# Weight tiles of their own, modulation weights on two queues, and three w1 loads moved ahead of the value copies

## The chip, the cores and the metric

The kernel runs on one core of a Trainium2 chip. The metric is device time in microseconds of one execution. The engines are named as in the profile: PE (TensorE matmul) and PEld (its weight loads), DVE (VectorE), ACT (ScalarE), POOL (GpSimd) and SP (SyncE, which issues nearly all DMAs of this kernel).

## What is computed

One block with adaptive layernorm: S = 2048 tokens of D = 512 features in bfloat16, a local attention with 32 heads of 16 features whose window has 8 positions with a step of 2, and an MLP that mixes tokens, with F = 1792.

```python
mod = (_silu(c) @ w_mod).reshape(c.shape[0], 6, 1, -1)   # sa, ca, ga, sb, cb, gb
h = _layernorm(x) * (1 + ca) + sa
x = x + ga * _A_ref(h, A_wqkv, A_wo)
h = _layernorm(x) * (1 + cb) + sb
x = x + gb * _B_ref(h, B_w1, B_b1, B_w2, B_b2)

# _A_ref: q, k, v from x @ wqkv;  idx = pos - [0, 2, ..., 14], masked where negative
logits = jnp.einsum('bhsd,bhswd->bhsw', q, kg) * scale
o = jnp.einsum('bhsw,bhswd->bhsd', _softmax(logits), vg)      # then @ wo
# _B_ref: u = gelu(einsum('bsd,sf->bdf', layernorm(x), w1) + b1);  y = einsum('bdf,fs->bds', u, w2) + b2
```

## The kernel before

The tokens are worked in four chunks of 512 (`build_chunk`, chunk 0 to 3), each of four tiles of 128 tokens. Of each chunk: layernorm (statistics on DVE, then `rstd`: a logarithm into `lv` and an exponential into `rs` on ACT, then `nb` on DVE, then `n_sb`, on DVE or ACT), a transpose on PE, the modulation of the transposed tile into `hTb` (named hT below; its columns `sacol` and `a1col` come from matmuls with one column each on the modulation weights), then 48 matmuls for query, key and value with the weights as stationary operand. Their results are evicted from PSUM into `q_sb`, `k_c` and `v_c` by ACT or DVE.

The attention multiplies elementwise on DVE: four products `prod` of query and shifted key of each chunk, and four products `pvb` of the softmax weights `a2sb` and the value. For the latter the values lie four times in `vD`, shifted; 16 DMAs of 32 x 2104 elements copy them there out of `v_c` in each chunk, 8 of each half. `vD` has three buffers. The sums over features and positions are matmuls with constant matrices (`group`, `stack`). Then come the output projection, the residual, a second and a third layernorm, and `h3`.

The MLP's first matmuls take w1 in seven blocks of 256 columns (`fc` 0 to 6) and in two levels: level 0 works with the tokens of chunks 0 and 1 and parks its sums in `gT`, level 1 with chunks 2 and 3. A block of one level is 512 KB. Level 0 loads them in turn into four buffers `wst`, which first hold the modulation rows; so its blocks 4 to 6 are loaded when blocks 0 to 2 have been used. Level 1 takes dead space: `w_raw`, `hTb`, and two of `wst`. The second matmuls take w2 in eight blocks of 896 KB, loaded into dead attention buffers.

All loads but one go through SP's queue, which works in order. A wait of one DMA on its buffer holds all that stand behind it.

Nothing here is written in the order in which it runs. Each step is an operation of a graph with engines, durations and dependences; a planner (`_Graph.schedule`) walks through it with a model of the engines and of one DMA pipe, chooses among ready operations by a table of priorities (`PRI`, a number for each kind of step and chunk), and between ACT and DVE by the earlier end, with a penalty `DB` on DVE. The code is then written in that order. Every instruction is recorded at one helper line, L208, so that the profile's groups are told apart by tile names.

The weights for query, key and value lie in one tile, columns `t * D` to `(t + 1) * D` of each of four rows of blocks:

```python
w_raw = T([P, KT, 3 * D], BF, "w_raw")
load(w_raw[:, :, t * D:(t + 1) * D], wqkv_view[:, :, t * D:(t + 1) * D], ...)
lhsT = _ap(w_raw[:, kt, t * D + j: t * D + j + 1], [[4, P]])
```

Key and query loads are held by a tiny copy on DVE (`hold_w`) until the statistics of a token tile are there. PE runs 13 matmuls on a constant (`warm`) at the start.

Of the kernel before, what the change touches and what calls it, by code (L numbers as in the profile page):

```python
# [9 lines left out]
BF = mybir.dt.bfloat16  # L10
# [3 lines left out]
P = 128  # L14
# [243 lines left out]
def kernel(  # L258
# [13 lines left out]
    PRI=(("ln1s", (-13773, -14814, 4735, 3582)), ("rstd1", (-14433, 1324, -6172, 2750)),  # L272
         ("nb1", (-13688, -10031, 8315, 26112)), ("ln1n", (12276, 4360, 29028, 55658)),
         ("tr", (-27269, -16160, 5273, -11182)), ("hT", (-31581, -17745, 20709, -3603)),
         ("qkvk", (-10761, -39897, -10907, 28658)), ("qkvq", (36465, 12433, 33335, 19673)),
         ("qkvv", (23004, -1542, 56675, 39121)), ("evk", (-39675, -52214, -12496, 12715)),
         ("evq", (-2536, -6788, 16753, 3144)), ("evv", (13543, -6355, 34438, 27036)),
         ("khalo", (5854, -5148, 3210, 20138)), ("vhalo", (13698, 20720, 49158, 39104)),
         ("vd", (9675, -10333, 32741, 40101)), ("qk", (6637, 9160, 33741, 41660)),
         ("red", (-7058, -688, 36723, 23347)), ("max", (-21689, -24379, -17972, 13331)),  # L280
         ("sub", (-28150, -8660, 6329, 38993)), ("exp", (-23987, -14379, 2772, 8798)),
# [15 lines left out]
    DB: float = 0.4,  # L297
# [4 lines left out]
    WARM: int = 13,  # L302
# [5 lines left out]
    G.XLAT = 0.06  # L308
    C = 512
# [16 lines left out]
    def T(shape, dtype, name):  # L326
        return sb.tile(shape, dtype, name=name)
# [13 lines left out]
    w_raw = T([P, KT, 3 * D], BF, "w_raw")  # L341
# [98 lines left out]
    dma(wmodA, wmod_view[:, :, 0:2 * D], 2 * D * D * 2, [], vdk[0], "ld_wmodA")  # L440
# [10 lines left out]
    def load_w(t):  # L451
        load(w_raw[:, :, t * D:(t + 1) * D], wqkv_view[:, :, t * D:(t + 1) * D], D * D * 2, [], [("w", t)], f"ld_w{t}")

    def later_loads():

        for (t, st) in ((1, 1), (0, 3)):
            add("dve", 0.07, lambda t=t, st=st: nc.vector.tensor_copy(w_raw[:, 0, t * D:t * D + 1],
                                                                      mv[0][0][:, st, 0:1]),
                reads=[("mv0", 0, st)], writes=[("w", t)], name=f"hold_w{t}", lat=0.1, pk=-200.0)
            load_w(t)  # L460
# [125 lines left out]
    def build_chunk(ch):  # L586
# [82 lines left out]
        for (t, j0, j1) in plan:  # L669
# [3 lines left out]
            def f(t=t, j0=j0, n=n, sq=sq):  # L673
                for jj in range(n):
                    j = j0 + jj
                    for kt in range(KT):
                        lhsT = _ap(w_raw[:, kt, t * D + j: t * D + j + 1], [[4, P]])
# [19 lines left out]
        for hfd in range(2):  # L697
# [4 lines left out]
            for dh2 in range(2):  # L702
                for w4 in range(4):
# [4 lines left out]
                        [("vD", vs, w4, dh2)], f"vd{ch}_{hfd}{w4}{dh2}", rate=220.0)  # L708
# [190 lines left out]
    ctr_ws = [0]  # L899
# [149 lines left out]
```

## Time and profile before

| | us |
|---|---|
| median of 3 runs | 228.72 (228.63 to 230.21) |
| profiled execution | 229.2 |
| its span, first to last instruction | 227.2 |
| PE busy | 201.3 (89%) |
| DVE busy | 164.3 (72%) |
| ACT busy | 112.7 (50%) |
| mean granted clock of PE | 0.962 |

The profiled execution lies 2.0 us above its span. Times of rows are counted from the span's start. Busy time of PE is that of records whose ends are modelled, and matmuls overlap, so a busy PE may still do less than it could; a row's time of several matmuls divided by their number is the better measure. In a row with "idle before", the idle time is that of its engine, and the name behind the arrow is what the profile holds for the cause.

### The profile page before, as it was taken

How to read it: one execution, taken by the hardware profiler on the slowest of the kernel's cores; microseconds unless marked ns; L12 is line 12 of the kernel's file. 1: busy time of each engine (PE TensorE's matmuls, PEld its weight loads, DVE VectorE, ACT ScalarE, POOL GpSimd, SP SyncE). 2: the span in 40 equal slices, each digit the busy share in tenths (PEclk: the TensorE clock that was granted, in tenths of full speed). 3: DMA queues.
4: the chain of work that ended last, by engine and by line, in shares of the span. 5: the costliest groups of instructions: out<-in, count | busy, mean ns of one | idle time of the engine just before them, and what ended most of it. 6: DMA issues, size and time to landing. Idle time of an engine off the chain costs nothing.

```text
span 227.2 us, 3338 instructions
## 1 busy us (share of the span) xinstructions
PE 201.3 (89%) x1267; PEld 92.1 (41%) x1288; DVE 164.3 (72%) x225; ACT 112.7 (50%) x208; POOL 4.0 (2%) x27
## 2 busy tenths in 40 slices
PE   6639999979599999948999957999999999999993
PEld 2314553444245343413344313444444444444452
DVE  4562799998899999999995758996643344555444
ACT  2423985095987979773575924895653200000000
POOL 7000000000000000000000000000000000000000
PEclk9956999999999999976999999999999999999999
DMA  4899777899640000019999999999992011011111
GB/s 153 273 357 288 227 154 129 171 165 225 170 122 0 3 0 0 3 52 165 162 165 243 190 248 278 292 290 290 293 248 74 23 49 46 29 40 46 49 46 46
DMA packets 41555, 32.96 MB, mean 145 GB/s; under 512 B 1988, under 2 KB 38980, under 8 KB 41540
## 3 DMA queue, kind: packets, MB, share of 16 engines
q1 hardware_dynamic: 41532, 32.75, 61.1%
q8 instruction: 10, 0.16, 0.4%
q14 instruction: 5, 0.04, 0.1%
q10 hardware_dynamic: 8, 0.00, 0.0%
HBM read 22.03 MB, written 2.10 MB: 106 GB/s over the span
## 4 chain that ended last, share of the span: by engine, by line
PE 38%; DVE 16%; DMA 10%; issue 2%; SPq 0%; DVEq 0%
PE ps L208 38%; DMA vD<-v_c 10%; DVE pvb L208 6%; DVE h L208 3%; DVE prod L208 2%; DVE st L208 2%; DVE nm L208 1%; DVE mv L208 0%; SPq L208 0%; DVE k_c L208 0%; DVE va L208 0%; DVEq L208 0%; DVE nb L208 0%
## 5 line engine op out<-in xcount | busy, mean ns | idle before, releaser
L208 PE MATMUL ps<-hTb,w_raw 128*128 128x512 bf16 x184 | 46.1, 395 | 4.4 <-DVE st L208 2.3
L208 DVE TENSOR_TENSOR pvb<-a2sb,vD 128x4096 bf16<-128x4096 bf16 x16 | 36.0, 2288 | 7.9 <-DMA vD<-v_c 4.2
L208 PEld LDWEIGHTS <-w_raw 128*128 128x128 bf16 x240 | 25.9, 112 | 33.1 <-issue 8.5
L208 PE MATMUL ps<-h,wst 128*128 128x512 bf16 x139 | 33.8, 392 | 3.0 <-ACT h L208 2.2
L208 DVE TENSOR_TENSOR prod<-q_sb,k_c 128x4096 bf16<-128x4096 bf16 x16 | 36.0, 2285 | 0.0
L208 PEld LDWEIGHTS <-wst 128*128 128x128 bf16 x144 | 13.9, 100 | 22.0 <-issue 7.9
L208 PE MATMUL ps<-gT,vD 128*128 128x512 bf16 x82 | 18.2, 379 | 0.1
L208 PE MATMUL ps<-woq,o_sb 128*128 128x512 bf16 x63 | 16.2, 379 | 0.0
L208 PEld LDWEIGHTS <-vD 128*128 128x128 bf16 x132 | 10.5, 97 | 14.0 <-DMA vD<-in_w_mod_dram 2.0
L208 DVE SCALAR_TENSOR_TENSOR q_sb<-ps,b2col,gb_bc 128x512 f32<-128x512 f32 x8 | 6.0, 751 | 12.6 <-PE ps L208 12.6
L208 DVE SCALAR_TENSOR_TENSOR k_c<-ps,b2col,gb_bc 128x512 f32<-128x512 f32 (+1 forms) x9 | 6.2, 692 | 11.4 <-PE ps L208 11.4
L208 PEld LDWEIGHTS <-o_sb 128*128 128x128 bf16 x106 | 10.3, 98 | 9.9 <-issue 0.4
L208 PE MATMUL ps<-pvb,stack 128*32 128x512 bf16 x128 | 9.9, 384 | 4.1 <-DVE pvb L208 4.1
L208 PE MATMUL ps<-prod,group 128*32 128x512 bf16 x128 | 10.1, 398 | 2.7 <-DVE prod L208 2.5
L208 PE MATMUL ps<-gT,prod 128*128 128x512 bf16 x55 | 12.3, 379 | 0.1
L208 DVE BATCH_NORM_STATS2 st<-xx 128x6 f32<-128x512 bf16 x16 | 10.7, 671 | 2.1 <-DMA xx<-in_A_x_dram 2.1
L208 PE MATMUL ps<-gT,pvb 128*128 128x512 bf16 x55 | 12.2, 379 | 0.1
L208 ACT ACTIVATE k_c<-ps 128x1024 bf16<-128x1024 f32 (+1 forms) x9 | 8.3, 925 | 7.9 <-PE ps L208 7.8
L208 DVE BATCH_NORM_STATS2 st<-h 128x6 f32<-128x512 bf16 x16 | 10.9, 679 | 0.0
L208 PE MATMUL ps<-h,w_raw 128*128 128x512 bf16 x48 | 10.8, 379 | 0.0
L208 ACT ACTIVATE xx<-ps 128x512 bf16<-128x512 f32 x16 | 9.4, 587 | 2.3 <-PE ps L208 1.6
L208 ACT ACTIVATE v_c<-ps 128x1024 bf16<-128x1024 f32 x8 | 8.0, 1017 | 4.6 <-PE ps L208 3.2
(95 smaller groups left out, 242.7 us busy)
## 6 DMA issues: line engine op xcount, KB each, us to landing
vD<-v_c SPq DMA_DIRECT2D x64, 131.5 KB, 5.4
wst<-in_B_w_dram SPq DMA_DIRECT2D x9, 512.0 KB, 7.5
vD<-in_B_w_dram SPq DMA_DIRECT2D x3, 896.0 KB, 10.6
wst<-in_w_mod_dram SPq DMA_DIRECT2D x4, 512.0 KB, 8.5
prod<-in_B_w_dram SPq DMA_DIRECT2D x2, 896.0 KB, 9.8
pvb<-in_B_w_dram SPq DMA_DIRECT2D x2, 896.0 KB, 8.7
w_raw<-in_A_wqkv_dram SPq DMA_DIRECT2D x3, 512.0 KB, 4.8
xx<-in_A_x_dram SPq DMA_DIRECT2D x3, 512.0 KB, 7.7
```

What stands on the lines that cost most here:

```text
L208: r = fn(*a, **k)
```

## The change

Each of the three weights gets a tile of its own (`w_q`, `w_k`, `w_v`). The first load of modulation weights is cut in two halves of 512 KB: one stays in SP's queue, the other is issued on ACT's. The copies that hold the key and query loads are put first on DVE. Level 0's w1 blocks 4 to 6 are loaded into `w_q`, `w_k` and `w_v`, after the last query, key and value matmuls; level 1 takes `wst` for blocks 0 to 3, `hTb` for 4 and 5 and `w_q` for 6. There are 15 warm-up matmuls instead of 13. All of the priorities have new values, DVE's penalty falls from 0.4 to 0.2, and the planner's model of DMAs gets a longer fixed time and a lower rate of value copies.

```diff
-    PRI=(("ln1s", (-13773, -14814, 4735, 3582)), ("rstd1", (-14433, 1324, -6172, 2750)),
+    PRI=(("ln1s", (-62333, -28891, -1164, 11138)), ("rstd1", (-33229, 4350, 3857, 26221)),
...
-    DB: float = 0.4,
+    DB: float = 0.2,
...
-    WARM: int = 13,
+    WARM: int = 15,
...
+    G.DMA_FIXED = 2.2
...
-    w_raw = T([P, KT, 3 * D], BF, "w_raw")
+    w_p = [T([P, KT, D], BF, f"w_{n}") for n in "qkv"]
...
-    dma(wmodA, wmod_view[:, :, 0:2 * D], 2 * D * D * 2, [], vdk[0], "ld_wmodA")
+    dma(wmodA[:, 0:2, :], wmod_view[:, 0:2, 0:2 * D], 2 * D * P * 2 * 2, [], vdk[0][4:], "ld_wmodA", "act",
+        behind=[G.ops[-1]])
+    dma(wmodA[:, 2:4, :], wmod_view[:, 2:4, 0:2 * D], 2 * D * P * 2 * 2, [], vdk[0][:4], "ld_wmodB")
...
-        load(w_raw[:, :, t * D:(t + 1) * D], wqkv_view[:, :, t * D:(t + 1) * D], D * D * 2, [], [("w", t)], f"ld_w{t}")
+        load(w_p[t][:], wqkv_view[:, :, t * D:(t + 1) * D], D * D * 2, [], [("w", t)], f"ld_w{t}")
...
-            add("dve", 0.07, lambda t=t, st=st: nc.vector.tensor_copy(w_raw[:, 0, t * D:t * D + 1],
+            add("dve", 0.07, lambda t=t, st=st: nc.vector.tensor_copy(w_p[t][:, 0, 0:1],
                                                                       mv[0][0][:, st, 0:1]),
-                reads=[("mv0", 0, st)], writes=[("w", t)], name=f"hold_w{t}", lat=0.1, pk=-200.0)
+                reads=[("mv0", 0, st)], writes=[("w", t)], name=f"hold_w{t}", lat=0.1, pk=-1e6)
...
-                        lhsT = _ap(w_raw[:, kt, t * D + j: t * D + j + 1], [[4, P]])
+                        lhsT = _ap(w_p[t][:, kt, j:j + 1], [[4, P]])
...
-                        [("vD", vs, w4, dh2)], f"vd{ch}_{hfd}{w4}{dh2}", rate=220.0)
+                        [("vD", vs, w4, dh2)], f"vd{ch}_{hfd}{w4}{dh2}", rate=170.0)
...
-            if last and fc < 5:
...
-                w = ctr_ws[0] % NWS
-                ctr_ws[0] += 1
-                w1p = wst[w][:, 0:nst, :]
-                wk, w = [("wst", w)], ("wst", w)
+            spare = (fc - 4 if fc >= 4 else None) if not last else {4: 3, 5: 4, 6: 0}.get(fc)
+            if spare is None:
+                w1p, wk = wst[fc][:, 0:nst, :], [("wst", fc)]
+            else:
+                src_ = w_p[spare][:].rearrange("p a b -> p (a b)") if spare < 3 else (
+                    hTb[:, spare - 3, :, :].rearrange("p a b -> p (a b)"))
+                w1p = src_.rearrange("p (a b) -> p a b", b=EW)[:, 0:nst, :]
+                wk = [("w", spare)] if spare < 3 else [("hT", spare - 3, kt) for kt in range(KT)]
...
-                behind=last_vd[-16:] if last else (), after=last_qkv[-6:] if last and fc < 5 else (), rate=290.0)
+                behind=last_vd[-16:] if last else (), after=last_qkv[-6:] if spare is not None else (), rate=290.0)
```

Three places in the order of the built program. Buffer numbers are shifted by two by the new tiles. First DVE at the start, from the end of the first chunk's statistics to its first modulated tiles (`hTb`); before:

```order
L208 SCALAR_TENSOR_TENSOR nb_0_138<-mv_0_122,rs_0_132 128x2
L208 CAST w_raw<-mv_0_122 128x1 x2
L208 COPY vD_89<-sc 128x512
L208 SCALAR_TENSOR_TENSOR nb_0_138<-mv_0_122,rs_0_132 128x2
L208 COPY sacol<-ps_63 128x4
L208 TENSOR_SCALAR a1col<-ps_63 128x4
L208 TENSOR_SCALAR n_sb<-xx,rs_0_132,nb_0_138 128x512 x2
L208 TENSOR_SCALAR hTb<-ps_64,a1col,sacol 128x512 x2
```

The same place after the change, from the third tile's statistics on:

```order
L208 CAST w_k<-mv_0_124 128x1
L208 BN_STATS st_0_120<-xx 128x6
L208 BN_AGGR mv_0_124<-st_0_120 128x2
L208 SCALAR_TENSOR_TENSOR nb_0_140<-mv_0_124,rs_0_134 128x2
L208 CAST w_q<-mv_0_124 128x1
L208 TENSOR_SCALAR n_sb<-xx,rs_0_134,nb_0_140 128x512 x2
L208 SCALAR_TENSOR_TENSOR nb_0_140<-mv_0_124,rs_0_134 128x2
L208 COPY vD_91<-sc 128x512
L208 COPY sacol<-ps_63 128x4
L208 TENSOR_SCALAR a1col<-ps_63 128x4
L208 TENSOR_SCALAR hTb<-ps_64,a1col,sacol 128x512 x2
```

DVE's two normalizations move from behind the copies of the modulation columns to ahead of them, and the copies that hold the key and query loads stand apart and earlier.

Second ACT, from the first chunk's normalizations to the second chunk's `lv`, `rs` and `n_sb`; before:

```order
L208 ACTIVATE n_sb<-xx,nb_0_138,rs_0_132 128x512 x2
L208 ACTIVATE hTb<-ps_61,sacol,a1col 128x512 x2
L208 ACTIVATE k_c_74<-ps_62 128x512
L208 ACTIVATE k_c_74<-ps_63 128x512
L208 ACTIVATE k_c_74<-ps_64 128x2x512
L208 ACTIVATE q_sb_72<-ps_61 128x512
L208 ACTIVATE k_c_75<-k_c_74 128x4x16
L208 ACTIVATE lv_1_127<-mv_1_123,epscol 128x4
L208 ACTIVATE rs_1_133<-lv_1_127 128x4
L208 ACTIVATE n_sb<-xx,nb_1_139,rs_1_133 128x512 x3
```

After the change:

```order
L208 ACTIVATE n_sb<-xx,nb_0_140,rs_0_134 128x512 x2
L208 ACTIVATE hTb<-ps_61,sacol,a1col 128x512 x2
L208 ACTIVATE k_c_76<-ps_62 128x512
L208 ACTIVATE k_c_76<-ps_63 128x512
L208 ACTIVATE k_c_76<-ps_64 128x2x512
L208 ACTIVATE k_c_77<-k_c_76 128x4x16
L208 ACTIVATE lv_1_129<-mv_1_125,epscol 128x4
L208 ACTIVATE rs_1_135<-lv_1_129 128x4
L208 ACTIVATE v_c_78<-ps_61 128x2x512
L208 ACTIVATE n_sb<-xx,nb_1_141,rs_1_135 128x512 x4
```

The query eviction (`q_sb`) between the key evictions and the second chunk's `lv` is gone from there, and a value eviction stands behind `rs`.

Third SP's queue around the value copies of chunks 2 and 3 (`vD<-v_c`; `wst`, `w_raw` and `w_q` to `w_v` from in_B_w are w1 blocks); before:

```order
L208 DMA vD_88<-v_c_77 32x2104 x8
L208 DMA vD_89<-v_c_76 32x2104 x8
L208 DMA vD_90<-v_c_76 32x2104 x8
L208 DMA vD_88<-v_c_77 32x2104 x7
L208 DMA wst_96<-in_B_w_dram 128x8x256
L208 DMA vD_88<-v_c_77 32x2104
L208 DMA wst_97<-in_B_w_dram 128x8x256
L208 DMA vD_89<-v_c_77 32x2104 x6
L208 DMA wst_98<-in_B_w_dram 128x8x256
L208 DMA vD_89<-v_c_77 32x2104 x2
L208 DMA w_raw<-in_B_w_dram 128x8x256 x3
```

After the change:

```order
L208 DMA vD_90<-v_c_79 32x2104 x8
L208 DMA w_q<-in_B_w_dram 128x8x256
L208 DMA w_k<-in_B_w_dram 128x8x256
L208 DMA w_v<-in_B_w_dram 128x8x256
L208 DMA vD_91<-v_c_78 32x2104 x8
L208 DMA vD_92<-v_c_78 32x2104 x8
L208 DMA vD_90<-v_c_79 32x2104 x8
L208 DMA vD_91<-v_c_79 32x2104 x8
L208 DMA wst_98<-in_B_w_dram 128x8x256
```

Three w1 loads move from between the copies of chunk 3 to ahead of the copies of chunk 2. The first row of each piece is the second half of chunk 1.

## Rows read from the trace of the kernel before

**Rows 1.** Windows, four stages: length, PE, PEld, DVE, ACT, POOL busy, clock, DMA share, GB/s.

```profile
0.00:23.80 23.80, 16.22 (x88) 7.30 (x90) 10.13 (x32) 8.55 (x17) 4.03 (x27) 0.78 0.88 272
23.80:111.00 87.20, 77.40 (x597) 36.30 (x605) 84.45 (x96) 63.73 (x113) 0.00 (x0) 0.96 0.52 104
111.00:138.00 27.00, 22.56 (x182) 8.93 (x187) 20.00 (x12) 15.23 (x29) 0.00 (x0) 1.00 1.10 211
138.00:223.50 85.50, 85.11 (x407) 39.62 (x408) 48.84 (x84) 25.16 (x51) 0.00 (x0) 1.00 0.51 135
```

**Rows 2.** Timeline of the start: start us, us, engine, operation [idle before <-releaser].

```profile
7.17 0.92 SPq L208 DMA_DIRECT2D w_raw<-in_A_wqkv_dram  x2
...
7.51 1.50 ACT L208 ACTIVATE n_sb<-xx,nb,rs 128x512 bf16<-128x512 bf16 x2
...
9.13 0.95 PE L208 MATMUL ps<-sc,vD 128*128 128x1 bf16 x32 [1.54 <-DMA vD<-in_w_mod_dram]
...
10.12 0.16 DVE L208 COPY sacol<-ps 128x4 f32<-128x4 f32 x1 [2.32 <-PE ps L208]
...
10.26 0.73 DVE L208 TENSOR_SCALAR n_sb<-xx,rs,nb 128x512 bf16<-128x512 bf16 x2
...
12.01 1.45 ACT L208 ACTIVATE hTb<-ps,sacol,a1col 128x512 bf16<-128x512 bf16 x2 [3.00 <-PE ps L208]
...
13.05 0.59 PE L208 MATMUL ps<-hTb,w_raw 128*128 128x512 bf16 x1 [1.08 <-DMA w_raw<-in_A_wqkv_dram]
...
15.97 0.15 PEld L208 LDWEIGHTS <-w_raw 128*128 128x128 bf16 x2 [2.84 <-DMA w_raw<-in_A_wqkv_dram]
...
17.56 0.18 DVE L208 BATCH_NORM_AGGREGATE mv<-st 128x2 f32<-128x6 f32 x1
...
21.72 1.02 ACT L208 ACTIVATE k_c<-ps 128x1024 bf16<-128x1024 f32 x1 [1.93 <-PE ps L208]
22.64 0.59 ACT L208 ACTIVATE q_sb<-ps 128x512 bf16<-128x512 f32 x1
23.11 0.26 ACT L208 ACTIVATE k_c<-k_c 128x64 bf16<-128x64 bf16 x1
23.26 0.30 ACT L208 ACTIVATE lv<-mv,epscol 128x4 f32<-128x4 f32 x1
...
23.83 0.16 DVE L208 SCALAR_TENSOR_TENSOR nb<-mv,rs 128x4 f32<-128x4 f32 x1 [5.29 <-ACT rs L208]
```

**Rows 3.** Windows of the start, columns as in rows 1.

```profile
7.60:10.40 2.80, 1.27 (x40) 1.25 (x40) 0.44 (x4) 1.41 (x3) 0.00 (x0) 1.00 0.75 245
10.40:20.60 10.20, 6.36 (x22) 2.50 (x21) 5.50 (x14) 2.64 (x4) 0.00 (x0) 0.50 1.11 327
```

**Rows 4.** Timeline of PE, the last w1 blocks.

```profile
167.94 7.07 PE L208 MATMUL ps<-h,wst 128*128 128x512 bf16 x32
```

**Rows 5.** Timeline of DVE, the last four value products.

```profile
124.56 4.50 DVE L208 TENSOR_TENSOR pvb<-a2sb,vD 128x4096 bf16<-128x4096 bf16 x2 [2.71 <-ACT a2sb L208]
130.97 2.29 DVE L208 TENSOR_TENSOR pvb<-a2sb,vD 128x4096 bf16<-128x4096 bf16 x1 [1.91 <-DMA vD<-v_c]
135.54 2.29 DVE L208 TENSOR_TENSOR pvb<-a2sb,vD 128x4096 bf16<-128x4096 bf16 x1 [2.28 <-DMA vD<-v_c]
```

**Rows 6.** SP's queue: two w1 loads; issue to landing of wst, 110 to 180 us.

```profile
125.35 0.53 SPq L208 DMA_DIRECT2D wst<-in_B_w_dram  x1
...
149.40 3.04 SPq L208 DMA_DIRECT2D wst<-in_B_w_dram  x1
...
DMA to landing us min/median/max: 8.6/10.2/11.7
```

**Rows 7.** Windows around the value copies, columns as in rows 1.

```profile
90.00:99.00 9.00, 7.01 (x43) 3.27 (x44) 8.76 (x16) 7.56 (x17) 0.00 (x0) 1.00 0.01 2
...
103.00:115.00 12.00, 11.44 (x85) 4.62 (x86) 11.90 (x16) 5.19 (x8) 0.00 (x0) 0.88 1.05 160
136.00:146.00 10.00, 8.06 (x43) 3.56 (x43) 9.09 (x16) 6.12 (x16) 0.00 (x0) 1.00 1.09 282
```

More of the change, by code (lines that the diff above doesn't have):

```diff
@@ L271 @@
     out: bass.AP,
-    PRI=(("ln1s", (-13773, -14814, 4735, 3582)), ("rstd1", (-14433, 1324, -6172, 2750)),
[L273 to L281, printed above, removed]
[11 rows of a table removed]
+    PRI=(("ln1s", (-62333, -28891, -1164, 11138)), ("rstd1", (-33229, 4350, 3857, 26221)),
+         ("nb1", (-35128, -10199, 606, 61630)), ("ln1n", (-13250, -779, 43561, 82136)),
+         ("tr", (-42262, -34195, 20572, -3461)), ("hT", (-50005, -19470, 30352, 9017)),
+         ("qkvk", (-4121, -22202, -18413, 51700)), ("qkvq", (32552, 14395, 18838, 32017)),
+         ("qkvv", (12501, 10460, 80919, 50056)), ("evk", (-22227, -27999, -13500, 34769)),
+         ("evq", (-21544, 751, 504, 4679)), ("evv", (33896, 8448, 60640, 52635)),
+         ("khalo", (3373, -999, 15697, 32477)), ("vhalo", (15160, 31777, 58416, 57816)),
+         ("vd", (15555, 6823, 48214, 59794)), ("qk", (15175, 12857, 42871, 54449)),
+         ("red", (4921, -7740, 48749, 42783)), ("max", (-40383, -24565, -6786, 7476)),
+         ("sub", (-31386, -8103, 37482, 40474)), ("exp", (-35480, -16607, -2144, 1231)),
[11 rows of a table added]
     MK: int = 1000,
@@ L897, in chained @@
         return op
-    ctr_ws = [0]
     bounds = [0] + list(LEVELS) + [NST]
@@ L909 @@
         for fc in range(F // EW):
-            if last and fc < 5:
-                w = ("wr", fc)
-                src_, off = (w_raw, fc * 2048) if fc < 3 else (hTb, (fc - 3) * 2048)
-                w1p = src_[:].rearrange("p a b -> p (a b)" if fc < 3 else "p a b n -> p (a b n)")[
-                    :, off:off + nst * EW].rearrange("p (a b) -> p a b", a=nst)
-                wk = [("w", fc)] if fc < 3 else [("hT", fc - 3, kt) for kt in range(KT)]
-                w = wk[0]
-            else:
-                w = ctr_ws[0] % NWS
-                ctr_ws[0] += 1
-                w1p = wst[w][:, 0:nst, :]
-                wk, w = [("wst", w)], ("wst", w)
+            spare = (fc - 4 if fc >= 4 else None) if not last else {4: 3, 5: 4, 6: 0}.get(fc)
+            if spare is None:
+                w1p, wk = wst[fc][:, 0:nst, :], [("wst", fc)]
+            else:
+                src_ = w_p[spare][:].rearrange("p a b -> p (a b)") if spare < 3 else (
+                    hTb[:, spare - 3, :, :].rearrange("p a b -> p (a b)"))
+                w1p = src_.rearrange("p (a b) -> p a b", b=EW)[:, 0:nst, :]
+                wk = [("w", spare)] if spare < 3 else [("hT", spare - 3, kt) for kt in range(KT)]
+            w = wk[0]
             dma(w1p, w1_view[:, s_lo:s_hi, fc * EW:(fc + 1) * EW], P * nst * EW * 2, [], wk, f"ld_w1_{li}_{fc}",
-                behind=last_vd[-16:] if last else (), after=last_qkv[-6:] if last and fc < 5 else (), rate=290.0)
+                behind=last_vd[-16:] if last else (), after=last_qkv[-6:] if spare is not None else (), rate=290.0)
             sm = G.slot("ps")
```

22 rows, old and new, of the table PRI are left out of this document.

## The prediction

> **What bounds the kernel now.** I read the windows view first, because a share of busy time over the whole span mixes stages with different limits. The reader is to see four stages [rows 1]. Up to 23.8 us nothing is full: PE is busy for 16.22 us, at a mean granted clock of 0.78, and DVE for 10.13. From 23.8 to 111 DVE is busy for 84.45 of 87.2 us: it is the bound. From 111 to 138 neither is full (PE 22.56 and DVE 20.00 of 27), while the DMA engines are. From 138 on PE is busy for 85.11 of 85.5 us at full clock. So a gain must come from the first stage, which sets when the DVE stage begins, or from the third, which sets when the last matmuls may begin; what is saved there moves everything behind it, as long as DVE and PE find their inputs.
>
> Then the timeline of the start [rows 2], for what ends last. The first query-key-value matmul starts at 13.05 behind a DMA into w_raw, and the next weight load waits for another one until 15.97. SP issued the key and the query weights from 7.17, then a part of x, then the value weights. While the clock is low the DMA moves 327 GB/s [rows 3], 1.6 us for each of these 512 KB loads. If the wait at 13.05 is for the second (query) load, the key weights had landed at 11.4; two loads later, at 16.2, the value weights land, which is where the second wait ends. So the key matmuls wait for weights that they don't read: all three lie in one tile, and the column sets of the three interleave in it. What follows is a chain on ACT, which works in order: the third key eviction at 21.72, a query eviction, the halo copy, and only at 23.26 the logarithm for the second chunk's layernorm, whose statistics DVE had ready at 17.74. DVE idles 5.29 us for it, until 23.83.
>
> Last, DVE at the end of the attention [rows 5]: its last two value products wait 1.91 and 2.28 us for value copies (vD<-v_c). SP's queue [rows 6] has three w1 loads between those copies; the last of them, at 125.35, is shown.
>
> **The change, part by part.**
>
> *Start, term A.* Three edits work on it. The normalizations of tiles 2 and 3 stood on DVE behind the copy of the modulation columns (10.12, then 10.26) and now stand on ACT, which doesn't wait for those columns. They can begin there when DVE has done the two other tiles (0.73 us, in the place of ACT's two from 7.51) and the second bias step, near 8.3, and take 1.50: done at 9.8. The transposes then follow the modulation matmuls, which end at 10.08, without a break: 16 in some 1.2 us, and the last two hT on ACT, 1.45 us in before, end near 12.8 instead of 13.46. The key tile is there by then (11.4), so the 16 key matmuls run from about 12.4 with no wait. At full clock (2.4 GHz) one takes 0.22 us, 32 of them 7.07 [rows 4], so they end at 15.9; at 1.2 GHz they take 0.44 each and end at 19.4. In before the third eviction could start at 21.72. From there to the logarithm go 0.92 us of the eviction and 0.15 of the halo copy's step; the query eviction between them is now later in ACT's order. So the logarithm could start at 17.1 (full clock) or 20.5 (low clock), against 23.26. It can't start ahead of the second chunk's statistics, which are done at 17.74 if x lands as now, and up to some 0.9 us earlier if the loads, whose two holding copies now come earlier on DVE, move up. So A is between 5.5 and 6.2 at full clock, 2.8 at the low one. I take 6.0, for the full clock: the low one began at 10.4 after a stretch with 1.27 us of PE work in 2.8 [rows 3], and this stretch is now shortened from both sides, by two more warm-up matmuls ahead and by earlier transposes behind.
>
> A must not be lost again in the DVE stage. DVE has 84.45 us of work there; by the order of the changed kernel it takes on one more query eviction (0.69) and one hT (0.53), and gives up three normalizations of 0.4 and one more of h: nothing, within 0.4 us. The new table of priorities moves many other instructions between neighbouring places, but on an engine without idle time that changes no sum.
>
> *Modulation weights on two queues.* The DMA of 1 MB lands just before 9.13. It is now two halves; the one on ACT is issued behind the table load, that is near 2.7 instead of 1.8 us. I count nothing: the trace has no such split, and the bounds are -0.9 us (the late issue is paid in full) and +1.5 (PE's idle time before 9.13 goes). The Trainium skill, "DMA: Bandwidth & Descriptors", section "Issuing engines are not separate DMA queues", says that transfers from several issuing engines share the same 16 DMA engines, so that a second queue saves only issue time. By that rule this part gives nothing, by the hope behind a second queue it would give the 1.5.
>
> *Three w1 loads out of the value copies, term B.* Loads of w1 and w2 alone move 282 GB/s, value copies alone 160 GB/s, both with the DMA share over 1 [rows 7]. A w1 load of 512 KB is then 1.86 us, three are 5.6; a value copy of 32 x 2104 elements is 0.84. The copies of the last two chunks run as one full stretch, so without the three loads the last ones land 5.6 us earlier. The two waits of DVE, 1.91 + 2.28 = 4.19, are shorter than that and go; then DVE itself is late next, with four products of 2.29 us in a row. B is 4.2. The wait of 2.71 us before the first of the four is for ACT's copy of the attention weights and stays.
>
> The loads go into the tiles of the query, key and value weights. SP now issues them ahead of the copies of chunk 2, and everything behind them in SP's queue waits with them: the value copies of chunks 2 and 3. The last matmuls that read the query and key tiles come before the last value matmuls of chunk 2, on which those copies wait anyhow, so only the third load (1.86 us) can stand in their way, and the DMA is idle there: 2 GB/s from 90 to 99 us [rows 7]. I count 0; if the cover is gone, 1.9 us to all of B.
>
> *The last stage.* It has the same matmuls. One load is read earlier than before: the fourth w1 block of the second half. In before its place in SP's queue (issued at 149.40) was that of the sixth block. It takes part in rival 3.
>
> **Sum.** The profiled execution has a span of 227.2 us and took 229.2; the median of the three runs is 228.72, so the profile is 0.5 us above it, less than I can resolve. 229.2 - 6.0 - 4.2 = 219.0 us.
>
> **The rivals.**
>
> 1. *The clock falls at the start all the same.* For: the modulation matmuls have one column each and the transposes are short, and in before just this work let the clock go from 1.00 to 0.50 [rows 3]. Against: the pause gets shorter. A is 2.8 instead of 6.0: 222.2 us.
>
> 2. *The loads are still in the way of the copies.* If the value tile comes free late, or SP is held at the first load, all 5.6 us lie ahead of chunk 2's copies instead of within chunk 3's. The last copy lands as before relative to the DVE work, B is 0: 223.2. Against it stands the idle DMA.
>
> 3. *The fourth w1 block comes late, and it gets slower.* In before, 32 matmuls were left when PE came to the last two blocks at 167.94 [rows 4]; in the new order 56 are left when it comes to the fourth, so this point is at 167.94 - 24 x 0.22 - 10.2 = 152.4. Its place in SP's queue was issued at 149.40, and such loads took 8.6 to 11.7 us from there to landing [rows 6]. If place and time don't move, it lands at 159.6 in the median, and PE waits 7.2 us in the one stage where it is the bound. There the clock would fall as at the start: 10.2 us at 0.50 [rows 3] is 5.1 us of matmuls. Together 12.3: 231.3. The price begins with a landing at 152.4, and from 157.5 on the kernel is slower than before. Against it: the queue ahead is shorter by the three loads (5.6) and starts earlier by A, so the load should land near 148, with 4 us in hand.
>
> 4. *The change doesn't free the key matmuls.* If the wait until 15.97 was truly for the key weights, the 16 matmuls begin there and end at 19.5, as at low clock: A is 2.7 and the time 222.3.
>
> **How the numbers follow.** The forecast has 0.60, rival 1 0.22, rival 2 0.09, rival 3 0.03, rival 4 0.06. The likeliest case gives 219.0. The range reaches down to 229.2 less 7.7 (A with the 1.5 of an earlier modulation) less 4.2 less the 0.5 between profile and median, 216.8, and up past rivals 1, 2 and 4 to 224.0, which leaves room for 1 to 2 us of lost cover in two of them. About 1% is what a measurement of this kernel can tell from no change, 226.4 to 231.0. Only rival 3, and rivals 1 and 2 together with more lost cover, come near it: faster 0.94, same 0.04, slower 0.02.
>
> **What would show it.** A is right if the key matmuls start before 13 us and run through, if no DMA into a weight tile is named before them, and if DVE's 5.29 us are gone, so that the first value product starts some 6 us earlier. The clock in the stretch from 10 to 21 us tells the forecast from rival 1. B is right if the last four value products follow each other without a DMA wait; rival 2 if such waits show at chunk 2's or the last ones; rival 3 if PE waits for a DMA into wst after its last attention work. The forecast is wrong if DVE is found idle between 20 and 110 us by more than the 2.8 us of now, for then the new order has starved it and A is lost in the middle.

## The result, and the profile after

The changed kernel took 221.99 us in the median of four executions (221.25 to 226.06), beside 229.47 us (228.63 to 231.53) of the kernel before. The forecast of 219.0 is 3.0 us too low, and its range of 216.8 to 224.0 holds the result. A fifth execution took 220.20. Some executions were disturbed (the first profile of the changed kernel at 226.06 us, three of the eight with the loads back, at 226.60, 230.57 and 521.05, and two of the four with 13 warm-up matmuls, 223.69 and 223.56) and are left out of ratios and comparisons. The ratio to the kernel before is 0.9634, with a 95% interval of 0.9548 to 0.9719. The same kernel was run once more beside the experiments: 219.80 us (219.49 to 222.07) against 229.44, ratio 0.9602 (0.9528 to 0.9675). Its eight executions of the two runs lie between 219.49 and 222.31, with 220.7 in their middle. Where a run is compared with the changed kernel below, both 219.80 and 220.7 are given where it matters: the intervals of its two runs reach 1.7 and 2.0 us to either side, so a difference of 1 us between two medians can't be told from nothing.

The rows below are of the second profile, an execution of 219.78 us with a span of 217.8.

Windows of the changed kernel, columns as in [rows 1]. They are cut at the same events as before: the `nb` after the wait on ACT, the first value product of chunk 2, and 0.2 us after the end of the last value product.

```profile
0.00:18.00 18.00, 13.94 (x91) 7.04 (x93) 10.03 (x32) 8.53 (x17) 4.04 (x27) 1.00 0.85 271
18.00:105.00 87.00, 76.16 (x591) 35.21 (x600) 84.19 (x95) 64.54 (x114) 0.00 (x0) 0.96 0.60 142
105.00:128.60 23.60, 22.99 (x181) 9.12 (x183) 19.98 (x13) 16.15 (x30) 0.00 (x0) 1.00 1.09 208
128.60:214.10 85.50, 85.13 (x409) 39.74 (x414) 47.96 (x84) 25.52 (x51) 0.00 (x0) 1.00 0.48 125
```

Beside [rows 1] the four stages are 18.0 instead of 23.8, 87.0 instead of 87.2, 23.6 instead of 27.0, and 85.5 as before. That is 5.8 from the first and 3.4 from the third stage, 9.4 in all with the 0.2 of the second, and the span fell by just that, from 227.2 to 217.8. DVE's idle time in the second stage is 2.8 us as before, so nothing of the first gain was lost on the way. The clock of 0.96 in that stage is a fall to 0.50 from 95 to 102 us, behind a stretch in which PE had little to do (1.9 us of work from 90 to 96); the kernel before has it from 99 to 106, every other profile somewhere between 92 and 109, and the prediction doesn't speak of it.

Timeline of the start, columns as in [rows 2]:

```profile
1.44 0.41 ACTq L208 DMA_DIRECT2D vD<-in_w_mod_dram  x1
...
7.47 1.19 PE L208 MATMUL ps<-sc,vD 128*128 128x1 bf16 x32
...
10.56 4.09 PE L208 MATMUL ps<-hTb,w_k 128*128 128x512 bf16 x15 [0.41 <-DVE hTb L208]
...
14.00 0.69 DVE L208 BATCH_NORM_STATS2 st<-xx 128x6 f32<-128x512 bf16 x1 [3.04 <-DMA xx<-in_A_x_dram]
...
15.41 3.64 PE L208 MATMUL ps<-hTb,w_v 128*128 128x512 bf16 x16 [0.76 <-DMA w_v<-in_A_wqkv_dram]
...
17.33 0.30 ACT L208 ACTIVATE lv<-mv,epscol 128x4 f32<-128x4 f32 x1 [1.33 <-DVE mv L208]
...
18.01 0.13 DVE L208 SCALAR_TENSOR_TENSOR nb<-mv,rs 128x4 f32<-128x4 f32 x1
```

The key matmuls start at 10.56 and run through. The logarithm starts at 17.33, and what it waits for now is DVE's statistics, no longer ACT's own queue; they in turn began at 14.00, after 3.04 us of waiting for x. The 5.29 us ahead of `nb` are gone. Where the clock was 0.50 before [rows 3], it is 1.00 now, with PE busy for 9.07 us of the same window instead of 6.36:

```profile
10.40:20.60 10.20, 9.07 (x39) 4.46 (x40) 6.88 (x20) 6.94 (x12) 0.00 (x0) 1.00 1.06 298
```

DVE's value products of the last two chunks, to be read beside [rows 5]:

```profile
111.21 4.49 DVE L208 TENSOR_TENSOR pvb<-a2sb,vD 128x4096 bf16<-128x4096 bf16 x2 [0.35 <-PE ps L208]
119.47 8.90 DVE L208 TENSOR_TENSOR pvb<-a2sb,vD 128x4096 bf16<-128x4096 bf16 x4 [3.16 <-ACT a2sb L208]
```

The last four follow each other without a DMA wait. The wait for the softmax weights ahead of them has grown from 2.71 to 3.16, and a wait of 0.35 for PE is new: 4.19 - 0.45 - 0.35 = 3.4, what the third stage lost. The name ACT hides an engine behind it: ACT copies the weights right behind an eviction (`o_sb`) for which it waited on PE, and PE's matmuls follow each other nearly without a break there.

```profile
117.50 1.02 ACT L208 ACTIVATE o_sb<-ps 128x1024 bf16<-128x1024 f32 x1 [1.89 <-PE ps L208]
118.42 1.02 ACT L208 ACTIVATE a2sb<-ps 128x1024 bf16<-128x1024 f32 x1
```

### The profile page after: what moved, and what is told of

It reads as the page before. It is cut to its first block, busy times and chain, and to the rows that moved or that the text cites. A ratio compares the mean times of both kernels' runs of the same rounds, so it can differ in the third digit from the quotient of the medians.

```text
span 224.1 us, 3367 instructions
## 1 busy us (share of the span) xinstructions
PE 202.9 (91%) x1290; PEld 91.6 (41%) x1290; DVE 163.2 (73%) x223; ACT 115.0 (51%) x210; POOL 4.0 (2%) x27
## 4 chain that ended last, share of the span: by engine, by line
PE 49%; DVE 12%; issue 2%; ACT 2%; DVEq 0%
PE ps L208 49%; DVE pvb L208 5%; DVE h L208 3%; DVE prod L208 2%; DVE st L208 1%; ACT a2sb L208 1%; DVE nm L208 0%; ACT o_sb L208 0%; DVE k_c L208 0%; ACT h L208 0%; DVE mv L208 0%; DVE va L208 0%; DVE nb L208 0%; DVEq L208 0%
## 5 line engine op out<-in xcount | busy, mean ns | idle before, releaser
L208 PE MATMUL ps<-h,wst 128*128 128x512 bf16 x128 | 31.8, 402 | 3.4 <-ACT h L208 2.7
L208 PEld LDWEIGHTS <-wst 128*128 128x128 bf16 x128 | 12.7, 102 | 21.0 <-issue 8.8
L208 PE MATMUL ps<-hTb,w_k 128*128 128x512 bf16 x64 | 17.4, 421 | 0.6 <-DVE hTb L208 0.4
L208 PE MATMUL ps<-hTb,w_v 128*128 128x512 bf16 x64 | 15.1, 381 | 2.1 <-DMA w_v<-in_A_wqkv_dram 2.1
L208 PE MATMUL ps<-hTb,w_q 128*128 128x512 bf16 x64 | 15.1, 381 | 0.0
L208 DVE BATCH_NORM_STATS2 st<-xx 128x6 f32<-128x512 bf16 x16 | 10.8, 677 | 5.1 <-DMA xx<-in_A_x_dram 5.1
L208 PEld LDWEIGHTS <-w_q 128*128 128x128 bf16 x96 | 9.8, 109 | 11.3 <-issue 2.5
L208 PEld LDWEIGHTS <-w_k 128*128 128x128 bf16 x80 | 8.9, 116 | 11.9 <-issue 5.6
L208 ACT ACTIVATE k_c<-ps 128x1024 bf16<-128x1024 f32 (+1 forms) x9 | 8.3, 926 | 10.4 <-PE ps L208 10.4
L208 PEld LDWEIGHTS <-w_v 128*128 128x128 bf16 x80 | 8.4, 111 | 11.3 <-DMA w_v<-in_A_wqkv_dram 2.6
```

Of the source, the lines that this page charges most:

```text
L208: r = fn(*a, **k)
```

## The experiments

Unless said otherwise the order of the instructions is frozen at that of the kernel named, so that an edit changes what it says and nothing else. Each was timed beside the kernel before, whose medians were 229.39 to 229.69. The profiles have one thing in common: the span is the end of DVE's last value product plus nearly the same time. Ends and spans are of the profiled execution, which took 2.0 us more than its span; the medians are of all executions of the run, those with the loads back of five.

| kernel | median | last value product ends | span | difference |
|---|---|---|---|---|
| before | 229.4 to 229.7 | 137.83 | 227.2 | 89.4 |
| before, separate tiles | 225.61 | 134.33 | 223.6 | 89.3 |
| the same and loads ahead | 222.72 | 130.24 | 219.8 | 89.6 |
| changed | 219.80 | 128.37 | 217.8 | 89.4 |
| changed, one DMA for the modulation | 219.63 | 127.51 | 217.0 | 89.5 |
| changed, one weight tile | 224.05 | 131.48 | 220.9 | 89.4 |
| changed, w1 loads back | 222.55 | 131.95 | 221.1 | 89.2 |
| changed, x first, late copies | 218.53 | 126.46 | 215.9 | 89.4 |
| changed, x first | 219.03 | 127.71 | 217.2 | 89.5 |
| changed, 13 warm-up matmuls | 222.42 | 132.24 | 221.7 | 89.5 |
| changed, 12 matmuls out ahead | 220.08 | 127.17 | 216.6 | 89.4 |
| changed, 12 matmuls out behind | 219.13 | 130.29 | 218.0 | 87.7 |

The ends are a row's start plus its time, as 119.47 + 8.90 of the row above.

**The same kernel again.**

> The changed kernel once more, for a second profile of it. Theory (A and B as forecast): the logarithm of the second chunk starts between 17.1 and 19 us, DVE's wait of 5.29 us is gone, the first query-key product starts some 5 us earlier than the 33.0 of before, and the half clock seen from 29.7 to 36.5 us is absent, since it came from loads that landed late in that one execution; time 220 to 221.5. Rival (lost in the middle): PE waits for the modulation rows and its clock falls near 30 us in this execution too, the first product starts after 31 us; time 221.5 to 222.5.

It took 219.80, the logarithm came at 17.33 and the half clock near 30 us was absent. The first query-key product started at 28.96 instead of 33.02. The theory held in the main: the product came 4.1 us earlier, not some 5, and the time is 0.2 below what was expected. In the first profile x came at 15.46 and the modulation rows later still. PE waited for them, and behind that wait four matmuls took 1.89 us, against 1.04 for such four in the second profile: the clock fell there. DVE then waited for the last row. Three rows of the first profile:

```profile
15.46 0.69 DVE L208 BATCH_NORM_STATS2 st<-xx 128x6 f32<-128x512 bf16 x1 [4.25 <-DMA xx<-in_A_x_dram]
...
30.48 1.89 PE L208 MATMUL ps<-wst,vD 128*128 128x512 bf16 x4 [2.46 <-DMA wst<-in_w_mod_dram]
...
38.82 0.69 DVE L208 COPY gb_bc<-ps 128x512 f32<-128x512 f32 x1 [3.52 <-PE ps L208]
```

**One tile again, in the changed kernel.**

```diff
-    w_p = [T([P, KT, D], BF, f"w_{n}") for n in "qkv"]
+    w_raw = T([P, KT, 3 * D], BF, "w_raw")
+    w_p = [w_raw[:, :, t * D:(t + 1) * D] for t in range(3)]
```

> The changed kernel with query, key and value weights in one interleaved tile again; order, loads and queues as in the changed kernel (the spare w1 blocks go to regions of that tile). Theory (term A is the false wait): the key matmuls wait for the query load and for the value load, until 16 us, the logarithm of the second chunk comes 3 to 5 us later and the time is 3 to 6 us longer, 224.5 to 227.5. Rival (the start is bound by x and by the order of the instructions, not by the tile): under 1 us longer, although the false wait is back.

It took 224.05 us (222.90 to 224.81; ratio 0.9776, 0.9703 to 0.9849): 4.25 us above 219.80, 3.3 above 220.7, and 3.1 by the spans. The theory held. PE, DVE and the window of the start:

```profile
11.86 0.39 PE L208 MATMUL ps<-hTb,w_raw 128*128 128x512 bf16 x1 [1.83 <-DMA w_raw<-in_A_wqkv_dram]
14.76 1.47 PE L208 MATMUL ps<-hTb,w_raw 128*128 128x512 bf16 x3 [2.51 <-DVE st L208]
...
22.02 0.16 DVE L208 SCALAR_TENSOR_TENSOR nb<-mv,rs 128x4 f32<-128x4 f32 x1 [4.70 <-ACT rs L208]
...
10.40:20.60 10.20, 6.01 (x18) 2.53 (x20) 4.36 (x11) 2.66 (x5) 0.00 (x0) 0.67 1.10 309
```

The stops of the key matmuls are back (the second is put down to DVE's statistics, which no matmul of this row reads; it ends 1.5 us after x landed, at 13.23 in this run, as the wait for the value weights does in the changed kernel, 14.00 and 15.41), and `nb` is 4.0 us later. The clock falls too, at 12.1 us behind the first of the two stops, and is low until 18.9: a mean of 0.67. How much of the 4.0 us is the stops and how much the clock isn't shown.

**Separate tiles alone, in the kernel before.** The loads, holding copies and readers of the three parts go to `w_p[t]`, level 1's blocks 0 to 2 to `w_p[fc]`.

```diff
-    w_raw = T([P, KT, 3 * D], BF, "w_raw")
+    w_p = [T([P, KT, D], BF, f"w_{n}") for n in "qkv"]
```

> The kernel before with a tile for each of the three weights and nothing else; its order of instructions, its loads and its 13 warm-up matmuls stay. Theory (the false wait is the larger part of A): the key matmuls no longer stop until 15.97, the second chunk's logarithm comes 2.5 to 4.5 us earlier, DVE's 5.29 us shrink by that, and the time is 225 to 227. Rival (the order and the clock make A): the gap is filled, but the clock stays low from 10.4 us and the query eviction stands ahead of the logarithm as before; under 1.2 us, about 228.5.

It took 225.61 us (225.48 to 225.86; ratio 0.9817, 0.9773 to 0.9860): 4.1 us shorter, 3.6 by the spans. The theory held: the logarithm starts 4.8 us earlier than in [rows 2], `nb` follows at 19.02, and the waits at the end stand as in [rows 5], one of them put down to PE. The clock fell near 10.5 us as before, but rose again at 13.9 and not at 20.6:

```profile
10.40:20.60 10.20, 9.96 (x55) 5.35 (x51) 7.14 (x21) 6.07 (x11) 0.00 (x0) 0.83 1.09 311
...
18.46 0.30 ACT L208 ACTIVATE lv<-mv,epscol 128x4 f32<-128x4 f32 x1
...
18.99:107.80 88.81, 77.63 (x608) 36.19 (x606) 84.59 (x96) 63.80 (x114) 0.00 (x0) 0.98 0.54 119
...
127.53 2.29 DVE L208 TENSOR_TENSOR pvb<-a2sb,vD 128x4096 bf16<-128x4096 bf16 x1 [1.76 <-PE ps L208]
132.04 2.29 DVE L208 TENSOR_TENSOR pvb<-a2sb,vD 128x4096 bf16<-128x4096 bf16 x1 [2.22 <-DMA vD<-v_c]
```

The window shows a price. Between `nb` and chunk 2's first value product lie 88.8 us instead of 87.2: DVE idles 4.2 instead of 2.8. Two waits for PE are new, of 0.69 and 0.63 us: in the old order DVE's work there isn't always ready when it comes earlier. Of 4.8 us, 1.6 are lost in the middle.

**Separate tiles and the three loads ahead, in the kernel before.** The three loads stand ahead of chunk 2's copies, and level 0's blocks 4 to 6 have the tiles of the changed kernel. Level 1's blocks 0 to 2, which would meet them there, go to `wst`, block 6 to `w_q`:

```diff
+    mv_ = [o for o in order if o.name in ("ld_w1_0_4", "ld_w1_0_5", "ld_w1_0_6")]
+    order = [o for o in order if o not in mv_]
...
+    order[i:i] = mv_
```

> The kernel before with separate weight tiles and, besides, w1 blocks 4 to 6 of level 0 in them, their loads ahead of the second half of chunk 1's copies or of chunk 2's in SP's queue; order of all else as before. Theory (term B, in an order in which PE is less full): the two DVE waits of 1.91 and 2.28 are gone and the time is 3.5 to 4.5 us below the run with separate tiles alone. Rival (as measured from the other side): only 2 to 2.5 us below it.

It took 222.72 us (221.83 to 223.36; ratio 0.9687, 0.9636 to 0.9738), 2.9 us below separate tiles alone. In its profile both waits are gone and the last product ends 4.1 us earlier:

```profile
121.34 8.90 DVE L208 TENSOR_TENSOR pvb<-a2sb,vD 128x4096 bf16<-128x4096 bf16 x4 [2.89 <-ACT a2sb L208]
```

The span fell by 3.8, the median by 2.9; the median lies between what theory and rival gave. The middle stage is 88.8 us long as with separate tiles alone.

**The three loads back among the copies, in the changed kernel.** There are two runs; the rows are of the second.

```diff
+    vd3 = [o.idx for o in order if o.name.startswith("vd3_")]
+    for o, n in zip(mv_, (7, 8, 14)):
+        i = next(k for k, q in enumerate(order) if q.idx == vd3[n])
+        order.insert(i, o)
```

> The changed kernel with the three w1 loads put back in SP's queue among the value copies of chunk 3, at the places they had before (after the 7th, 8th and 14th of 16); tiles as in the changed kernel. Theory (term B): the last two value products wait for copies again, 4 us in all, and the time is 3.5 to 4.5 us longer, about 225.5. Rival (PE has had no idle time since 103 us and sets the end): the waits on DVE come back, but PE has w1 matmuls to do meanwhile, so the time is 0 to 2 us longer.

> The changed kernel with the three w1 loads back among chunk 3's value copies once more, for a profile of a typical execution: the first one gave 2.4 us more than the changed kernel (222.2 against 219.8) in the executions that can be compared, where term B says 4.2. Theory (B is 4.2 on DVE, but PE has w1 matmuls to do meanwhile): DVE waits for value copies by 4 us at its last two products, PE's idle time between 111 us and the end grows by only some 2.4, and the time is 2 to 3 us longer. Rival (the copies land sooner than I think): DVE's waits for copies are only 2 to 2.5 us.

Five executions took 221.92 to 224.76, with 222.55 in their middle (ratio of the second run 0.9725, 0.9634 to 0.9815). That is 2.7 us above the 219.80 of the run of the changed kernel, and 1.8 above the 220.7 of all its executions. The window of the start, PE's key matmuls, the logarithm, and DVE at the start and the end:

```profile
10.40:20.60 10.20, 9.69 (x36) 4.32 (x37) 6.18 (x17) 6.22 (x11) 0.00 (x0) 0.83 1.07 290
...
10.76 5.78 PE L208 MATMUL ps<-hTb,w_k 128*128 128x512 bf16 x16 [0.41 <-DVE hTb L208]
...
18.26 0.30 ACT L208 ACTIVATE lv<-mv,epscol 128x4 f32<-128x4 f32 x1 [0.37 <-DVE mv L208]
...
14.93 0.69 DVE L208 BATCH_NORM_STATS2 st<-xx 128x6 f32<-128x512 bf16 x1 [3.77 <-DMA xx<-in_A_x_dram]
...
121.25 6.70 DVE L208 TENSOR_TENSOR pvb<-a2sb,vD 128x4096 bf16<-128x4096 bf16 x3 [3.16 <-ACT a2sb L208]
129.66 2.29 DVE L208 TENSOR_TENSOR pvb<-a2sb,vD 128x4096 bf16<-128x4096 bf16 x1 [1.72 <-DMA vD<-v_c]
```

One wait is back, not two, and it is 1.72 us: the rival was right in kind, the copies land sooner for DVE, and the wait is still shorter than it gave. Their last one lands at 129.6, where before it landed at 135.5 [rows 5], 5.9 us later, while DVE comes to its last four products only 3.3 us earlier. By the time, 1.8 to 2.7 us, the first run's rival (0 to 2) is nearer than its theory. So in the changed order the separate loads take away 1.7 us of waiting; the other 2.5 of the 4.2 had already gone. Most of what else parts the two profiles is this one's later start: x came 0.9 us later, the first product, at 30.21, 1.2.

The start of this profile shows something else: with tiles of their own and no stop, the clock fell all the same, to 0.50 from 12.0 to 15.4 us, and the 16 key matmuls took 5.78 us. The logarithm still waited for DVE's statistics, so x set it and the low clock cost nothing there.

**The modulation weights in one DMA, in the changed kernel.**

> The changed kernel with the modulation weights in one DMA of 1 MB on SP's queue; all else in the changed order. Theory (the split is worth nothing, as the prediction counted): within 0.6 us of the changed kernel. Rival (two queues land the weights earlier): the modulation matmuls start 1.5 to 1.9 us later, near 9.1 instead of 7.3, the key matmuls and all behind them move with them, and the time is 1.5 to 1.9 us longer, about 223.

It took 219.63 us (219.03 to 220.86), the same within the spread. PE and DVE:

```profile
8.95 0.95 PE L208 MATMUL ps<-sc,vD 128*128 128x1 bf16 x32 [0.60 <-DMA vD<-in_w_mod_dram]
11.23 4.09 PE L208 MATMUL ps<-hTb,w_k 128*128 128x512 bf16 x15 [0.41 <-DVE hTb L208]
...
14.11 0.70 DVE L208 BATCH_NORM_STATS2 st<-xx 128x6 f32<-128x512 bf16 x1 [2.48 <-DMA xx<-in_A_x_dram]
```

The modulation matmuls start 1.5 us later without the split, the key matmuls 0.7, and the second chunk's x is where it was, 0.1 us apart. The start waits for x, so the time doesn't move: the rival's mechanism is there, its price is hidden.

**13 warm-up matmuls, in the changed kernel** (the loop's bound is 13 instead of `WARM`).

> The changed kernel with 13 warm-up matmuls instead of 15; all else in the changed order. Theory (the two more keep the clock up until the transposes, as term A took): the clock falls to half near 10 us as in the kernel before, the 16 key matmuls take up to twice 3.5 us, the logarithm moves from 17.3 to about 19 or 20 and the time is 1.5 to 3 us longer. Rival (the earlier transposes and the free key matmuls alone keep it up, and x sets the start): the clock stays at 1.00 until 24 us and the time within 0.6 us of the changed kernel.

The median of 222.42 (218.71 to 223.69) says little, since its executions lie 5 us apart. In the profile, of 223.69 us, the modulation weights came at 9.13 and the clock fell near 10.4 us, until 17.2. But x came at 17.59, and the logarithm, at 20.92, waited for DVE's statistics of it: x made this execution long, not the clock.

```profile
10.40:20.60 10.20, 8.95 (x37) 4.18 (x38) 4.29 (x12) 5.39 (x8) 0.00 (x0) 0.67 1.01 311
...
17.59 0.69 DVE L208 BATCH_NORM_STATS2 st<-xx 128x6 f32<-128x512 bf16 x1 [4.13 <-DMA xx<-in_A_x_dram]
...
20.92 0.30 ACT L208 ACTIVATE lv<-mv,epscol 128x4 f32<-128x4 f32 x1 [0.84 <-DVE mv L208]
```

All four profiles of kernels with 13 warm-up matmuls (before, both with separate tiles, this one) have the fall between 10.4 and 10.8 us, none of the nine with 15 has it there. With one DMA for the modulation weights they came nearly as late, at 8.95, and behind 15 warm-up matmuls the clock stayed at 1.00. So the profiles side with the theory on the clock. The shortest execution with 13, 218.71, had a mean clock of 0.990, that is 0.010 x 2 x 216.8 = 4.3 us at half clock in all; since every profile has at least 3.4 such us near 100, and the falls at the start last as long or longer, this one most likely had no fall at the start. It has no profile, and whether the two matmuls are worth any time stays open.

**12 matmuls left out.** Two runs leave out 12 of the 16 matmuls of one w1 block, some 2.6 us of PE work, ahead of the last value product (level 0's block 1) or behind it (level 1's block 1).

```diff
+                            if cut and 0 < i < nst - 1:
+                                continue
```

> The changed kernel without 12 of the 16 matmuls of level 0's w1 block 1 (its sums are left out; 2.65 us of PE work that lies ahead of the last value product, near 107 to 118 us). Theory (the span is the end of DVE's last value product plus what PE has queued behind it, 89.4 us in every profile so far): nothing, within 0.6 us. Rival (PE is the bound from 103 us on, 26.4 busy of 27 between 111 and 138): the 2.65 us are saved, time 217.2.

> The changed kernel without 12 of the 16 matmuls of level 1's w1 block 1 (its sums are left out; 2.65 us of PE work that lies behind the last value product). Theory (span is the last value product plus PE's queue behind it): 2.5 to 2.7 us shorter, 217.2. Rival (behind the last product PE has slack that a wait would fill): under 1.5 us.

Ahead: 220.08 us (218.63 to 221.16), which the median can't tell from nothing. The profile can: the last product ends 21.8 us after the start of chunk 2's first value product (105.38), in the changed kernel 23.1 after it (105.24). The wait of 0.35 is gone and that for the softmax weights is 2.27 instead of 3.16.

```profile
118.27 8.90 DVE L208 TENSOR_TENSOR pvb<-a2sb,vD 128x4096 bf16<-128x4096 bf16 x4 [2.27 <-ACT a2sb L208]
```

Beside that profile 1.3 of the 2.6 us came through, between theory and rival. How much of it is the cut isn't certain: seven profiles of the changed order without this cut have 22.0 to 23.4 us there, all longer, but the shortest only by 0.25. That one, with one DMA for the modulation, had the low clock ahead of the stage from 96.4 to 99.8 us only, the second profile from 95.0 to 101.8. Both point at the work that PE is behind with. Behind: 219.13 (217.76 to 220.33), 0.7 below 219.80 and 1.6 below 220.7, nearer to the rival than to the theory. Its profile had a late x (15.14), but the span was 87.7 us behind the last product instead of 89.4: 1.7 of the 2.6. Part of the rest is a new wait, for the last tokens' third layernorm; 0.4 us stay open.

```profile
150.02 7.25 PE L208 MATMUL ps<-h,wst 128*128 128x512 bf16 x31 [0.47 <-DVE h L208]
```

**x ahead of the value and query weights.** Since x sets the start, its load was moved right behind the key weights, in one run with the copies of the last modulation row and of the bias columns later on DVE, in the other without.

```diff
+    for k, n in zip(pos, ("ld_w1", "ld_x1", "ld_w2", "ld_w0")):
+        order[k] = ld[n]
```

> The changed kernel with the second chunk's x loaded right behind the key weights (then value, then query weights), and the copies of the last modulation row and of the bias columns on DVE moved behind the second and the third query-key product. Theory (the start is now bound by x on DVE, which waits 3.04 us for it until 14.0, and by 1.43 us for the last modulation row): x lands some 1.6 us earlier, both waits shrink, the attention ends 2 to 3 us earlier and the time is 217 to 218. Rival (PE is the bound from 103 us on): everything before moves, but the time falls by under 0.6 us.

> The changed kernel with the second chunk's x loaded right behind the key weights, without the later copies on DVE of the run that had both (that one was 1.3 us below the changed kernel, its last value product 1.9 us earlier). Theory (two waits in series: x, then the last modulation row): DVE starts on the second chunk near 12 instead of 14 us, but the wait for the last modulation row grows from 1.43 to some 3 us, and the time is within 0.6 us of the changed kernel. Rival (x alone sets the start): 1.3 to 2 us shorter.

With both it took 218.53 us (217.89 to 219.24; ratio 0.9508, 0.9461 to 0.9555), the lowest median of all; each of its executions is shorter than all eight of the changed kernel. Its theory asked for 217 to 218: the last product ends 1.9 us earlier, and the two waits were partly replaced by others. With x alone 219.03 (218.19 to 219.56; 0.9533, 0.9486 to 0.9579), between what theory and rival gave; whether the later copies add to it can't be told from 0.5 us. DVE in the run with x alone:

```profile
11.90 0.69 DVE L208 BATCH_NORM_STATS2 st<-xx 128x6 f32<-128x512 bf16 x1 [0.82 <-DMA xx<-in_A_x_dram]
16.41 0.69 DVE L208 BATCH_NORM_STATS2 st<-xx 128x6 f32<-128x512 bf16 x1 [1.23 <-DMA xx<-in_A_x_dram]
28.18 2.28 DVE L208 TENSOR_TENSOR prod<-q_sb,k_c 128x4096 bf16<-128x4096 bf16 x1
31.89 0.69 DVE L208 COPY gb_bc<-ps 128x512 f32<-128x512 f32 x1 [1.43 <-PE ps L208]
```

x lands 2.1 us earlier, the first product starts only 0.8 earlier: DVE now waits for the third chunk's x as well. The wait for the modulation row didn't grow, against the expectation. It is 1.43 us in this run, in the changed kernel and in three others, with x from 11.9 to 15.1. That fits PE's order, in which that row's matmuls follow 16 key matmuls, better than a landing; it wasn't tested.

## Why the prediction was right, and where it was off

**The start, A.** The mechanism was right: key matmuls that start before 13 us and run through, the logarithm at 17.33 within 17.1 to 17.74, full clock, and 5.8 us gained against 6.0. (By its own terms the lower of these two is 17.0: 15.9 + 0.92 + 0.15.) Of this, tiles alone make 4.8 in the old order (`nb` at 19.02), and putting the tile back costs 4.0 in the new; the rest is the order of the start. One sign was mis-stated: the first value product of all came 4.9 us earlier (51.69 instead of 56.62), not some 6; the 6.0 are there at chunk 2's (105.24 instead of 111.22).

**The clock.** The prediction laid the fall to a stretch with little PE work around the wait for the modulation weights and counted on the two warm-up matmuls and the earlier transposes to shorten it. The profiles agree as far as they go: with 13 warm-up matmuls the clock fell near 10.5 us also where the tiles were separate, so the false wait, which begins at 12.0 us in before, isn't what let it fall there. With the false wait the clock stayed low longer: until 20.6 us with it, until 13.9 and 14.2 without it in the same order. That is what the prediction left out, and why its low-clock case, A of 2.8, is too small: it kept the clock low through all 16 key matmuls, while separate tiles gave 4.8 though the clock fell. What sets the length isn't shown; with 13 warm-up matmuls in the changed order it lasted until 17.2.

**A in the middle.** The prediction held that the new table of priorities changes no sum on DVE. It compared before with after, and there it is right, 87.2 and 87.0. But the runs show that the sum would have changed without the table: with the old order the earlier start loses 1.6 us in the stage. The kernel with tiles and loads in the old order is 2.0 us above the 220.7 of all executions of the changed kernel, 2.9 above the 219.80, and the new order is probably a large part of that, by elimination: it was never tried alone. The split and the warm-ups are in it too; the split is worth nothing measurable by its own run, the worth of the warm-ups is open.

**The loads, B.** Both waits are gone; the term was mis-sized, 3.4 instead of 4.2, because the wait for the softmax weights grew by 0.45 and one of 0.35 for PE appeared. The prediction let the wait of 2.71 stay as it was. In the run with 12 matmuls less ahead both growths are gone (2.27, and no wait for PE), which points to PE being behind with its work; the sum has no term for that. The sum also gave all of B to the loads. In the old order they are worth 2.9 to 4.1, in the new one 1.7 (the wait) to 2.7: there DVE comes to its last four products 14.8 us after chunk 2's first instead of 13.3, and from the issue of the first copy to that of the last two pass 28.0 us instead of 29.2.

**The split.** Counted at nothing, and so it came: 219.80 us with two queues and 219.63 with one. The time agrees with the Trainium skill, "DMA: Bandwidth & Descriptors", section "Issuing engines are not separate DMA queues", by which issuing on a second engine saves only the time of issuing. The landing of the weights moved by more than that: the halves were issued at 1.44 and 1.81 and the one DMA at 1.81, but PE had them 1.5 us earlier. The estimate that ACT would issue its half near 2.7 was wrong: it issued at 1.44. The loads of the first x tiles took 3.4 us to land instead of 2.6 in the run with one DMA, and the key weights were issued 0.3 later. This is no accident of one pair: these loads took 2.6 to 3.0 us in the four profiles with one DMA and 3.1 to 4.5 in the nine with two.

**The rivals.** The clock at the start (rival 1), loads in the way (2), a late fourth block (3) and key matmuls that still wait (4) show in no row of the second profile. The fall at the start did come in the profile with the loads back (12.0 to 15.4 us), and cost nothing, since the logarithm waited for x. In the first profile the clock fell at another place, behind the wait for a modulation row.

**The 3 us of the median.** Of the typical execution, 219.78, the forecast missed 0.8: 0.2 of A and 0.8 of B, less the 0.2 that the second stage gave. The rest is the distance of other executions of the same kernel, up to 222.3 and, with the first profile, 226.06. The step of the prediction that bears on it is the one that read the limit of A as "if x lands as now". In before a late x was hidden, since DVE waited 5.29 us for ACT anyhow. Now DVE's start follows x: in the seven profiles with the changed start and x in its place, `nb` comes 4.0 to 4.7 us after the wait for x has ended, with x from 14.00 to 17.59. In the one with the latest x, that with 13 warm-up matmuls, x is 3.6 us later than in the second profile and the span 3.9 longer. So x moves the time. That it makes the spread of the executions isn't shown: the runs with x first lie within 1.4 us, but the executions of the kernel before, where x is hidden, lie as far apart (228.29 to 231.53) as those of the changed kernel.

## What to carry to other kernels

Data that arrive in several loads should have a tile for each, when their readers start at different times: here a wait for parts that weren't read cost 3 to 4 us, whatever low clock went with it included. When a wait is removed, look for the one behind it that it hid (here x), because the time now hangs on that one. Edits that shorten the same chain aren't additive: the loads were worth 2.9 us in one order and 1.8 to 2.7 in the other, and an earlier start was only kept whole where the order of the long stage fitted it. A wait is put down to the engine that came last; ask what that engine had waited for (here ACT for PE).

## What the hardware showed that was not expected

PE was busy for 97% of the stage ahead of the last value product (22.99 of 23.6 us), though the only waits of DVE there are one of 0.35 us for PE and one of 3.16 for ACT. With 2.6 us of PE's work left out the stage was 1.3 us shorter in the profile: a nearly full engine isn't the one that sets the whole end, but it can set a part of it under another engine's name. The medians, of executions 2.5 us apart, don't show it. The span minus the last product stayed at 89.2 to 89.6 us over all kernels that do the whole work behind it. And two queues of issue brought one transfer in 1.5 us earlier at the price of another, with the whole unchanged.
